# Recurrence on TensorE: a 64-column first half, a 64-partition second half, and two new step orders

## The chip, the cores and the metric

The kernel runs on one core of a Trainium2 chip. The metric is the device time of one execution in microseconds (us). The engines are named as the profile names them: PE (TensorE's matmuls) and PEld (its weight loads), DVE (VectorE), ACT (ScalarE), POOL (GpSimd) and SP (which issues the transfers).

## What is computed

A recurrence over 768 steps for 4 x 8 heads of size 40, then an attention mixture of experts, then a token and channel mixer. The change is in the recurrence:

```python
for t in range(S):
    y[:, :, t] = np.einsum('bhd,bhde->bhe', rt, state)
    Sa = np.einsum('bhde,bhe->bhd', state, at)
    state_decay = state * wt[:, :, None, :] - np.einsum('bhd,bhe->bhde', Sa, bt)
    state = state_decay + np.einsum('bhd,bhe->bhde', vt, kt)
```

## The kernel before, in words

The 768 steps are cut into 12 chunks of 64 steps, two chunks to a pair. The 32 heads lie in 11 groups of three (the last of two), and the groups in three quads (`QUADS`): 12, 12 and 8 heads. A step of the recurrence's program has a letter and a quad, for instance `z1`; in the text below a step of quad 1 is written z/1.

Inside a chunk the unknown row Sa depends on the rows before it, through a triangular 64x64 system for each head. It is solved in two halves of 32 rows. For one quad of one chunk the chain is:

- z (`z1`, line 275): old state times `a` into the PSUM tile `zu`, 64 partitions for the chunk's 64 rows; straight behind it the first t (`tv` with half 0, line 284): scores `sc` times values `vu`, added to rows 0 to 31. ACT then copies these rows, negated, into `zt0` (line 288).
- x (`xz`, line 297): the inverse of the diagonal block `xt` times `zt0`; ACT copies the result into `vu` (line 301). Below, x0 is the first half and x1 the second.
- t (`tv` with half 1, line 284): scores times values for rows 32 to 63, now with the first half's results in `vu`, called t1 below; ACT copies them into `zt1`; then x again for the second half.
- d (`ds`, lines 320 and 322): the new state into `ST`, which DVE writes (line 327), and s (`st`, line 336): its transpose.

In `vu` (128 partitions) one 64-partition half holds the chunk's values, the other one starts at zero (POOL memset, line 129) and takes the solved rows. The half of the solved rows is partitions 64 to 127 in even chunks and 0 to 63 in odd ones. A matmul writes 32 columns of the array for rows of one half, at array column 0 or 64 (first half) or 32 or 96 (second half); the heads of a quad alternate between the two sides (`sides`).

Beside this chain, PE makes the output of the chunk before: v (`vut`, line 361), r (`rs`, line 381), h (`hh`, line 351) and y (`yy`, line 394); scores c of the next pair (`scores`, line 204); k (`kbt`, line 251) and p (`ptt`, line 264). DVE masks the scores (lines 209 and 385), multiplies outputs (line 398), writes the state, makes the decays (`decay`, line 163 and others) and runs `solve`: a transpose into `tp` (line 225), 31 dependent double steps (lines 234 and 236) and a transpose into `xt` (line 239). `xt` of a pair is needed by the first x of the pair's even chunk, and `solve` can start when the last scores of that pair are masked and copied by ACT into `td` (line 217).

The strings `EVEN` and `ODD` (lines 34 and 35) give the order in which the steps of a chunk are emitted; the tile layer then places the instructions of all chunks on the engines, so the order on an engine is read from the built program. PSUM tiles come from small rings: three of `zu`, two each of `pm` and `psc`, one `y`.

Of the kernel before, what the change touches and what calls it, by code (L numbers as in the profile page):

```python
# [30 lines left out]
E = 40  # L31
FIRST = "p0 S p1 p2 L D k0 M V q0 q1 q2 k1 k2"
PN = (1, 1)
EVEN = "c0 c1 h0 v0 r0 v1 c2 z2 z0 D v2 y0 m1 x0 c3 z1 m2 s0 x1 x2 t0 r1 c4 c5 h1 t2 t1 y1 h2 r2 k0 k1 m0 c6 c7 x4 x3 c8 d0 c9 c10 c11 L s1 y2 d1 s2 x5 S k2 d2"
ODD = "h0 v0 z0 v1 A r0 x0 r1 y0 t0 h1 z1 M m2 v2 z2 x1 x3 y1 k0 r2 p0 x2 h2 p1 t1 m0 k1 k2 t2 L y2 x5 m1 s0 d0 p2 s2 s1 d2 x4 d1"
QUADS = [(0, 4), (4, 8), (8, 11)]

def sides(q, n):

    g0, g1 = QUADS[q]  # L40
    a, b, e = n * g0, n * (g0 + 2), min(n * g1, 32 if n > 1 else G)
    for i in range(b - a):
        yield a + i, 0, i
        if b + i < e:
            yield b + i, 1, i

def spans(q):

    g0, g1 = QUADS[q]
    return (0, 120 * g0, 240), (64, 120 * g0 + 240, min(120 * g1, 1280) - 120 * g0 - 240)  # L50
# [18 lines left out]
class Rec:  # L69
# [207 lines left out]
        s.tv(c, q, 0)  # L277

    def tv(s, c, q, half):
        nc = s.nc  # L280
        zu, sc, vu = s.T["zu", q], s.T["sc", c], s.T["vu", c]
        for h, b, i in sides(q, 3):
            o = 64 * b + 32 * half
            nc.tensor.matmul(zu[o:o + 32, 40 * i:40 * i + 40], sc[:, h, 32 * half:32 * half + 32],  # L284
                             vu[:, 40 * h:40 * h + 40], start=False, stop=True, skip_group_check=True)
        d = 64 * (1 - c % 2) + 32 * half
        for b, o, n in spans(q):
            nc.scalar.activation(s.zt[half][d:d + 32, o:o + n], zu[b + 32 * half:b + 32 * half + 32, :n], AF.Copy,  # L288
                                 scale=-1.0)
# [189 lines left out]
    def chunk(s, c):  # L479
# [34 lines left out]
        def solve():  # L514
            if even and p1:
                s.bg.append(s.solve(p + 1))

        def loads():
            s.rbd_load(c)
            if not last:  # L520
                s.load_r(c + 1)
            if c + 2 < 2 * n:
                s.load_chunk(c + 2)

        def load_next():
            if not even and p2:
                s.load_a(p + 2)
                s.load_kb(p + 2)

        def decay():  # L530
            if even and p2:
                s.bg.append(s.decay(p + 2))

        def scale():
            if not even and p2:
                while "pt" not in s.T[p + 2]:
                    s.pump(1)
                s.scale(p + 2)

        if even and p2:  # L540
# [4 lines left out]
                  S=lambda q: solve(), D=lambda q: decay(), L=lambda q: loads(), W=lambda q: c > 8 and next(s.cv, 0), A=lambda q: load_next(), M=lambda q: scale())  # L545
        for o in (EVEN if even else ODD).split():
            do[o[0]](int(o[1:] or 0))
# [590 lines left out]
```

## Time and profile before

| | us |
|---|---|
| median of 3 runs (lowest to highest) | 1063.22 (1062.9 to 1068.52) |
| profiled execution | 1056.61 |
| its span, first to last instruction | 1054.9 |
| recurrence within the span, to the last matmul of line 381 | about 451 |
| what follows (mixture of experts, mixers) | about 600 |

The recurrence is read by stages. A stage runs from the first x of one pair's even chunk to that of the next; these begin at 66.5, 163.3, 225.2, 290.8, 354.3 and 407.1 us of the span and are called stages 1 to 6 below. Stage 6 ends with the recurrence. The windows of the rows are cut a little earlier, where the transpose into `xt` starts. Matmuls in float32 stand as two records each in the trace, transposes as one.

### The profile page before, as it was taken

Reading aid. Unit: us, or ns where it says so; the run is one execution under the profiler, and the core shown is the slowest. Engines: PE = TensorE matmul, PEld = TensorE weight load, DVE = VectorE, ACT = ScalarE, POOL = GpSimd, SP = SyncE. Lnnn points to the kernel's source line nnn. Section 1 sums busy time; section 2 is a strip of 40 time slices with the busy share of each in tenths; the row PEclk is TensorE's granted clock in tenths of the full one; section 3 lists DMA queues with packets and bytes.
Section 4 is the critical chain, followed back from the end, with each engine's and each line's share of the span. In section 5 each row is a group of like instructions: output and inputs, shape, how many; then the busy total and the mean of one; then the engine's idle time right before and its main releaser. Section 6 shows DMA issues by size and latency. Waiting matters only on the chain.

```text
span 1054.9 us, 23653 instructions
## 1 busy us (share of the span) xinstructions
PE 944.2 (90%) x9378; PEld 814.6 (77%) x9378; DVE 675.0 (64%) x1793; ACT 481.9 (46%) x1250; POOL 169.7 (16%) x214
## 2 busy tenths in 40 slices
PE   2329889999999999967999999999998999999998
PEld 1327678887888888855877887888787898898887
DVE  6798697897988588648889777576287222222222
ACT  2225446646566565534667657666543121121211
POOL 5000000010000001343134142223254000000000
PEclk9758998999999999989999999999999999999999
DMA  9604424425243323465643441420262101101000
GB/s 175 133 2 95 102 49 107 91 79 133 50 105 79 97 61 99 138 196 137 159 116 89 124 115 31 98 61 26 86 203 63 56 1 56 34 21 56 1 25 25
DMA packets 101031, 88.84 MB, mean 84 GB/s; under 512 B 60785, under 2 KB 91073, under 8 KB 100321
## 3 DMA queue, kind: packets, MB, share of 16 engines
q1 hardware_dynamic: 100921, 87.34, 32.2%
q8 instruction: 74, 1.21, 0.5%
q14 instruction: 36, 0.29, 0.1%
HBM read 54.94 MB, written 15.73 MB: 67 GB/s over the span
## 4 chain that ended last, share of the span: by engine, by line
PE 65%; DVE 19%; DMA 7%; ACT 4%; issue 3%; SPq 2%; POOL 1%; DVEq 0%; ACTq 0%; POOLq 0%
PE pq L1031 11%; PE p L1045 11%; PE zu L284 3%; DVE pq L163 3%; PE psc L204 3%; PE psc L381 3%; PE po L858 3%; PE zu L297 3%; PE pq L832 2%; PE y L394 2%; PE pq L760 2%; PE pm L320 2%; PE pq L997 2%; PE pq L873 2%; PE pm L322 2%
## 5 line engine op out<-in xcount | busy, mean ns | idle before, releaser
L1035 DVE SCALAR_TENSOR_TENSOR hl<-pq,hh 128x512 fp32r<-128x512 f32 x72 | 49.6, 689 | 152.0 <-ACT hh L1034 152.0
L1034 ACT ACTIVATE hh<-pq 128x512 fp32r<-128x512 f32 x72 | 42.9, 596 | 190.9 <-PE pq L1031 190.9
L1045 PE MATMUL p<-c2h,hh 128*128 128x320 f32 x288 | 91.0, 316 | 3.4 <-DVE o L1048 3.4
L805 ACT ACTIVATE a<-s,nm 128x512 f32<-128x512 f32 (+3 forms) x128 | 68.7, 542 | 47.2 <-DVE nm L802 21.7
L1045 PE MATMUL p<-c2h,hl 128*128 128x320 f32 x288 | 89.5, 311 | 0.1
L1045 PE MATMUL p<-c2l,hh 128*128 128x320 f32 x288 | 89.4, 310 | 0.0
L297 PE MATMUL zu<-zt,xt 64*32 64x40 f32 x1536 | 43.2, 209 | 38.6 <-DVE pq L160 30.4
L301 ACT ACTIVATE vu<-zu 32x240 f32<-32x240 f32 (+1 forms) x144 | 48.5, 339 | 55.3 <-PE zu L297 45.6
L297 PEld LDWEIGHTS zu<-zt,xt 64*32 64x32 f32 x1536 | 37.3, 116 | 45.3 <-issue 37.0
L800 DVE TENSOR_REDUCE nm<-s 128x1 f32<-128x512 f32 (+3 forms) x128 | 61.9, 499 | 15.8 <-PE s L799 11.2
L288 ACT ACTIVATE zt<-zu 32x240 f32<-32x240 f32 (+1 forms) x144 | 48.6, 338 | 50.5 <-PE zu L284 48.8
L163 DVE TENSOR_TENSOR pq<-w,pq 120x88 f32<-120x88 f32 x186 | 61.0, 328 | 9.4 <-DMA w<-in_w 5.6
L818 POOL TENSOR_TENSOR a<-a,rs 128x128 f32<-128x128 f32 (+1 forms) x64 | 45.4, 731 | 126.6 <-DVE rs L813 90.6
L234 DVE TENSOR_TENSOR pr<-tp,x 128x31 f32<-128x31 f32 (+15 forms) x186 | 63.0, 339 | 3.9 <-DVE tp L225 0.5
L236 DVE TENSOR_TENSOR x<-x,pr 128x31 f32<-128x31 f32 (+15 forms) x186 | 63.3, 340 | 3.1
L1045 PEld LDWEIGHTS p<-c2h,hh 128*128 128x128 f32 x288 | 54.5, 189 | 7.7 <-DVE o L1048 5.0
L1031 PE MATMUL pq<-uh,c1h 128*128 128x512 f32 x144 | 57.5, 399 | 0.8 <-DVE ul L652 0.8
L1031 PE MATMUL pq<-uh,c1l 128*128 128x512 f32 x144 | 57.0, 396 | 0.0
L1045 PEld LDWEIGHTS p<-c2l,hh 128*128 128x128 f32 x288 | 54.5, 189 | 2.5
L1045 PEld LDWEIGHTS p<-c2h,hl 128*128 128x128 f32 x288 | 54.5, 189 | 0.3 <-DVE hl L1035 0.3
L204 PE MATMUL psc<-abd,kb 120*128 120x192 f32 (+1 forms) x242 | 51.1, 344 | 3.7 <-DVE sc L209 2.6
L284 PE MATMUL zu<-vu,sc 128*32 128x40 f32 x1536 | 50.8, 214 | 1.5 <-issue 0.8
(204 smaller groups left out, 2484.1 us busy)
## 6 DMA issues: line engine op xcount, KB each, us to landing
kb<-in_kb SPq DMA_DIRECT2D x5, 1320.0 KB
kh<-hb SPq DMA_DIRECT2D x64, 96.0 KB
cv<-in_c SPq DMA_DIRECT2D x18, 256.0 KB
w<-in_w SPq DMA_DIRECT2D x6, 660.0 KB
a<-in_a SPq DMA_DIRECT2D x6, 660.0 KB
r<-in_r SPq DMA_DIRECT2D x12, 330.0 KB
rbd<-in_r SPq DMA_DIRECT2D x36, 110.0 KB
vu<-in_v SPq DMA_DIRECT2D x12, 320.0 KB
```

Of the source, the lines that this page charges most:

```text
L163: e.tensor_tensor(two(pq, i + 1, x + 29 - 2 * i), two(t["w"], i, 31 - 2 * i), two(pq, i, x + 31 - 2 * i), OP.mult)
L204: nc.tensor.matmul(ps[:, n:n + nheads(g), :], t["kb"][:k, g, c % 2, :], abd[:k, g, :nheads(g), :], start=True, stop=True)
L234: v.tensor_tensor(prv, tp[:, j + 1:, j:j + 1].to_broadcast([128, n, j + 1]), x[:, j:j + 1, :j + 1].to_broadcast([128, n, j + 1]), OP.mult)
L236: v.tensor_tensor(x[:, j + 1:, :j + 1], x[:, j + 1:, :j + 1], prv, OP.subtract)
L284: nc.tensor.matmul(zu[o:o + 32, 40 * i:40 * i + 40], sc[:, h, 32 * half:32 * half + 32], vu[:, 40 * h:40 * h + 40], start=False, stop=True ...
L288: nc.scalar.activation(s.zt[half][d:d + 32, o:o + n], zu[b + 32 * half:b + 32 * half + 32, :n], AF.Copy, scale=-1.0)
L297: nc.tensor.matmul(zu[o:o + 32, 240 + 40 * i:280 + 40 * i], xt[r, h, :], s.zt[half][r, 40 * h:40 * h + 40], start=True, stop=True, skip_gr ...
L800: nc.vector.tensor_reduce(nm[:, x:x + 1], s, axis=AX.X, op=OP.max, negate=True)
L805: nc.scalar.activation(a[:, n0:n1], s, AF.Exp, bias=nm[:, -1:] if nb_ == 2 else nm[:, :1], accum_out=sm[:, x, i % 2:i % 2 + 1])
L1031: nc.tensor.matmul(p, l, r, start=(n == 0), stop=(n == 7))
L1035: nc.vector.scalar_tensor_tensor(hl, p, 0.0, hh, op0=OP.max, op1=OP.subtract)
L1045: nc.tensor.matmul(Y[s][i], hs[x][:, ts], w[:, k], start=(k + n == 0), stop=(k == 11 and n == 2))
```

## The change

`tv` with half 0 now multiplies all 64 columns of the scores, so it writes rows 0 to 63 of `zu` at once, over 128 partitions. The solved half of `vu` is zero at that time, so this adds the chunk's values for both halves. `tv` with half 1 then adds only what the solved first half gives to rows 32 to 63, over the 64 partitions that hold solved rows. The number of matmuls is the same. Both step orders are new.

```diff
-EVEN = "c0 c1 h0 v0 r0 v1 c2 z2 z0 D v2 y0 m1 x0 c3 z1 m2 s0 x1 x2 t0 r1 c4 c5 h1 t2 t1 y1 h2 r2 k0 k1 m0 c6 c7 x4 x3 c8 d0 c9 c10 c11 L s1 y2 d1 s2 x5 S k2 d2"
+EVEN = "m2 v0 h0 c0 z0 v1 c1 r0 c2 D v2 z2 x2 c3 m0 c4 x0 t2 z1 y0 x1 t1 c5 t0 h1 r1 r2 x3 y1 h2 c6 c7 k0 x5 c8 s0 c9 y2 x4 c10 c11 s2 d0 m1 S L d2 s1 k1 k2 d1"
...
     def tv(s, c, q, half):
...
+        u = 64 * (1 - c % 2)
+        r = slice(u, u + 64) if half else slice(0, 128)
+        m = 32 if half else 64
         for h, b, i in sides(q, 3):
             o = 64 * b + 32 * half
-            nc.tensor.matmul(zu[o:o + 32, 40 * i:40 * i + 40], sc[:, h, 32 * half:32 * half + 32],
-                             vu[:, 40 * h:40 * h + 40], start=False, stop=True, skip_group_check=True)
-        d = 64 * (1 - c % 2) + 32 * half
+            nc.tensor.matmul(zu[o:o + m, 40 * i:40 * i + 40], sc[r, h, 32 * half:32 * half + m],
+                             vu[r, 40 * h:40 * h + 40], start=False, stop=True, skip_group_check=True)
+        d = u + 32 * half
```

In the changed kernel lines 284, 297, 351, 381 and 394 are lines 288, 301, 355, 385 and 398, and `x` of the second half reads `zt_114`, of the first `zt_113`.

First place: PE at the start of an even chunk (chunk 4, counted from 0; its first x stands at 225.2 us in the trace before), from the first x on. Before:

```order
L297 MATMUL zu<-zt_113,xt 32x40 x32
L284 MATMUL zu<-vu,sc 32x40 x24
L351 MATMUL y<-S,r 64x120
L284 MATMUL zu<-vu,sc 32x40 x8
L351 MATMUL y<-S,r 64x80
L351 MATMUL y<-S,r 64x120
L297 MATMUL zu<-zt_114,xt 32x40 x12
L394 MATMUL y<-kbt,sr 64x40 x8
L297 MATMUL zu<-zt_114,xt 32x40 x20
L320 MATMUL pm<-vu,kbt 120x120
```

Now:

```order
L301 MATMUL zu<-zt_113,xt 32x40 x20
L288 MATMUL zu<-vu,sc 32x40 x8
L301 MATMUL zu<-zt_113,xt 32x40 x12
L355 MATMUL y<-S,r 64x120 x4
L385 MATMUL psc<-rbd,vut 128x192
L288 MATMUL zu<-vu,sc 32x40 x12
L385 MATMUL psc<-rbd,vut 128x192 x2
L288 MATMUL zu<-vu,sc 32x40 x12
L385 MATMUL psc<-rbd,vut 128x192 x2
L385 MATMUL psc<-rbd,vut 128x128
L398 MATMUL y<-kbt,sr 64x40 x12
L251 MATMUL pm<-ident,kb 128x120
```

The second half's t now starts between the x of the first half, output work of the chunk before stands between the links of the chain, and the first d comes later.

Second place: PE in the odd chunk behind it (chunk 5), around the z of quads 1 and 2. Before:

```order
L284 MATMUL zu<-vu,sc 32x40 x12
L275 MATMUL zu<-ST,a 64x120 x4
L284 MATMUL zu<-vu,sc 32x40 x12
L361 MATMUL pm<-ident,vu 120x128 x2
L351 MATMUL y<-S,r 64x120 x4
L361 MATMUL pm<-ident,vu 80x128
L275 MATMUL zu<-ST,a 64x120
L275 MATMUL zu<-ST,a 64x80
L275 MATMUL zu<-ST,a 64x120
L284 MATMUL zu<-vu,sc 32x40 x8
L297 MATMUL zu<-zt_113,xt 32x40 x12
```

Now:

```order
L275 MATMUL zu<-ST,a 64x120 x4
L288 MATMUL zu<-vu,sc 64x40 x12
L275 MATMUL zu<-ST,a 64x120
L275 MATMUL zu<-ST,a 64x80
L275 MATMUL zu<-ST,a 64x120
L288 MATMUL zu<-vu,sc 64x40 x8
L385 MATMUL psc<-rbd,vut 128x192 x4
L355 MATMUL y<-S,r 64x120
L301 MATMUL zu<-zt_113,xt 32x40 x8
L288 MATMUL zu<-vu,sc 32x40 x12
L301 MATMUL zu<-zt_113,xt 32x40 x12
```

The two z with their first t stand in a row and all write 64 rows, and a second half's t (32 rows) stands between two x.

Third place: DVE from the second transpose into `xt` on (163 us in the trace before). Before:

```order
L239 STREAM_TRANSPOSE xt<-x 128x32x32
L209 TENSOR_TENSOR sc<-psc,mask 128x384 x2
L163 TENSOR_TENSOR pq<-w,pq 120x2x44
L398 TENSOR_TENSOR ptt<-y,ptt 64x80
L163 TENSOR_TENSOR pq<-w,pq 120x2x44 x5
L165 TENSOR_TENSOR wp<-w,pq 120x44
L167 RECIPROCAL wr<-wp 120x44
L209 TENSOR_TENSOR sc<-psc,mask 128x384
L170 TENSOR_TENSOR pq<-pq,wr 120x22x32
L209 TENSOR_TENSOR sc<-psc,mask 128x384
L170 TENSOR_TENSOR pq<-pq,wr 120x22x32
L327 TENSOR_TENSOR ST<-pm,mf 120x480
```

Now, as far as the next transpose into `tp`:

```order
L239 STREAM_TRANSPOSE xt<-x 128x32x32
L209 TENSOR_TENSOR sc<-psc,mask 128x128
L163 TENSOR_TENSOR pq<-w,pq 120x2x44
L165 TENSOR_TENSOR wp<-w,pq 120x44
L167 RECIPROCAL wr<-wp 120x44
L170 TENSOR_TENSOR pq<-pq,wr 120x22x32 x2
L331 TENSOR_TENSOR ST<-pm,mf 120x480
L225 STREAM_TRANSPOSE tp<-td 128x1024
```

Most of the next pair's scores now stand ahead of this transpose into `xt`, inside the solve, and not behind it.

## Rows read from the trace of the kernel before

**Rows 1.** The page: busy time and share of the span; 40 equal slices, tenths.
```profile
PE 944.2 (90%) x9378; PEld 814.6 (77%) x9378; DVE 675.0 (64%) x1793; ACT 481.9 (46%) x1250; POOL 169.7 (16%) x214
PE   2329889999999999967999999999998999999998
```
**Rows 2.** Windows: stretch, its length, busy us (instructions) by engine, clock, DMA.
```profile
100.00:161.40 61.40, 53.28 (x704) 44.34 (x699) 49.61 (x139) 29.20 (x71) 2.70 (x4) 0.95 0.39 87
161.40:223.20 61.80, 59.97 (x944) 51.60 (x943) 50.46 (x135) 35.63 (x96) 3.82 (x6) 0.94 0.35 85
223.20:288.90 65.70, 62.11 (x992) 53.74 (x991) 55.95 (x149) 38.88 (x101) 4.57 (x6) 1.00 0.40 96
288.90:352.30 63.40, 61.06 (x978) 53.00 (x976) 53.18 (x132) 37.89 (x100) 3.82 (x6) 0.97 0.35 86
352.30:405.07 52.77, 51.41 (x909) 45.09 (x908) 38.11 (x98) 34.90 (x95) 2.27 (x3) 1.00 0.27 70
405.07:456.40 51.33, 47.74 (x853) 40.12 (x851) 33.71 (x61) 24.84 (x66) 16.15 (x10) 1.00 0.48 152
```
**Rows 3.** PE's waits: 100 to 161.4 us, then 161.4 to 288.9, then 288.9 to 405.
```profile
PE zu L297 <- issue: 2.5, 2, 1.8
PE y L351 <- DVE ptt L398: 1.9, 1, 1.9
...
PE zu L297 <- DVE xt L239: 1.8, 2, 1.1
...
PE zu L297 <- DVE xt L239: 2.1, 2, 1.6
```
**Rows 4.** Windows of two solves, from `tp` to the first x: columns as in rows 2.
```profile
122.00:163.00 41.00, 35.81 (x406) 30.27 (x406) 39.12 (x121) 15.65 (x38) 1.16 (x1) 0.95 0.22 52
241.00:291.00 50.00, 46.22 (x708) 39.19 (x710) 42.93 (x117) 27.57 (x74) 2.48 (x3) 1.00 0.43 98
```
**Rows 5.** Timeline of PE: start, length, line, tile, shape (rows*columns), records.
```profile
28.84 0.26 PE L284 MATMUL zu<-vu,sc 128*32 128x40 f32 x2
29.03 1.14 PE L204 MATMUL psc<-abd,kb 120*128 120x192 f32 x6
...
427.04 0.62 PE L297 MATMUL zu<-zt,xt 64*32 64x40 f32 x24
427.59 1.57 PE L381 MATMUL psc<-rbd,vut 120*128 120x192 f32 x8
429.09 0.90 PE L394 MATMUL y<-kbt,sr 128*64 128x40 f32 x24
429.91 0.62 PE L284 MATMUL zu<-vu,sc 128*32 128x40 f32 x24
430.47 0.63 PE L275 MATMUL zu<-ST,a 120*64 120x120 f32 x8
```
**Rows 6.** Timeline of PE, where neighbours have one shape and where not.
```profile
126.03 0.63 PE L351 MATMUL y<-S,r 120*64 120x120 f32 x8
126.50 0.85 PE L394 MATMUL y<-kbt,sr 128*64 128x40 f32 x24
...
134.28 0.63 PE L351 MATMUL y<-S,r 120*64 120x120 f32 x8
134.88 0.90 PE L336 MATMUL pm<-ident,ST 120*120 120x120 f32 x7
...
190.60 0.94 PE L297 MATMUL zu<-zt,xt 64*32 64x40 f32 x48
191.47 0.90 PE L394 MATMUL y<-kbt,sr 128*64 128x40 f32 x24
```
**Rows 7.** DVE: groups by line in 223.2 to 288.9 (busy us, mean ns).
```profile
L163 DVE TENSOR_TENSOR pq<-w,pq 120x88 f32<-120x88 f32 x32 | 10.7, 333 | 0.4
L209 DVE TENSOR_TENSOR sc<-psc,mask 128x384 f32<-128x384 f32 (+1 forms) x12 | 6.1, 512 | 0.7 <-PE psc L204 0.4
L398 DVE TENSOR_TENSOR ptt<-y,ptt 64x240 f32<-64x240 f32 (+1 forms) x12 | 4.5, 378 | 4.5 <-PE y L394 4.3
```

More of the change, by code (lines that the diff above doesn't have):

```diff
@@ L33 @@
 PN = (1, 1)
-EVEN = "c0 c1 h0 v0 r0 v1 c2 z2 z0 D v2 y0 m1 x0 c3 z1 m2 s0 x1 x2 t0 r1 c4 c5 h1 t2 t1 y1 h2 r2 k0 k1 m0 c6 c7 x4 x3 c8 d0 c9 c10 c11 L s1 y2 d1 s2 x5 S k2 d2"
-ODD = "h0 v0 z0 v1 A r0 x0 r1 y0 t0 h1 z1 M m2 v2 z2 x1 x3 y1 k0 r2 p0 x2 h2 p1 t1 m0 k1 k2 t2 L y2 x5 m1 s0 d0 p2 s2 s1 d2 x4 d1"
+EVEN = "m2 v0 h0 c0 z0 v1 c1 r0 c2 D v2 z2 x2 c3 m0 c4 x0 t2 z1 y0 x1 t1 c5 t0 h1 r1 r2 x3 y1 h2 c6 c7 k0 x5 c8 s0 c9 y2 x4 c10 c11 s2 d0 m1 S L d2 s1 k1 k2 d1"
+ODD = "A z0 x0 v0 v1 z1 z2 r0 h0 x2 t0 m1 x1 m2 s0 v2 r1 y0 h1 m0 r2 M y1 p0 L p1 p2 h2 y2 x3 t1 t2 d0 s2 k0 x5 s1 k1 x4 d2 k2 d1"
 QUADS = [(0, 4), (4, 8), (8, 11)]
```

## The prediction

> **What bounds the kernel now.** I read the page first: PE is busy 90% of the span, and the slices show it well short of full only in the first three, under 80 us, and mildly where the recurrence ends [rows 1]. The change touches the recurrence alone, so next come its stages, as windows [rows 2]: from 161 to 405 us PE is busy 234.6 of 243.7 us (the sum of four rows), so it bounds, with 9.1 us idle. From 100 to 161 us it idles 8.1 us. The waits tell for whom [rows 3]: the largest after "issue" are for outputs (line 398) and for `xt`, the end of the solve on DVE. So a second bound runs close behind: the solve. In the solve from 122 us DVE is busy 39.1 of 41.0 us, so DVE sets its end; in the one from 241 us it is busy 42.9 of 50.0 us, and PE 46.2 [rows 4]: the longest wait for `xt` there is 1.1 and 1.6 us [rows 3], so PE and the solve end nearly together. A change must be added up on PE, and then held against the solve.
>
> **Prices.** All from full-clock stretches. One float32 matmul of line 284 alone is two records, one behind the other, and with what surrounds it takes 0.19 us (28.84 to 29.03); 24 records, a quad on two sides of the array, take 0.56 us (429.91 to 430.47) [rows 5]. A quad is 12 slots of two records side by side (the last quad, 8 heads with 6 on one side, too), so a slot is (0.56 - 0.19)/10 = 0.037 us, and 0.12 us is constant. Line 394, the same 128 partitions and 40 columns but 64 columns of weights, takes 0.82 us (429.09 to 429.91): a slot of (0.82 - 0.12)/12 = 0.058. Line 297, 64 partitions and 32 columns, takes 0.55 us, like line 284 [rows 5]. The constant belongs to a change of tile shape: four heads of line 351 take 0.47 us when line 394 follows, which has its shape, and 0.60 us when full-width line 336 does [rows 6], so a change costs 0.13 us; I take 0.12. Other steps, by start to start or busy time: r and c 0.34 us a matmul (1.50 us for four, less one change), h 0.12, y 0.058, transposes (s, k) 0.12 [rows 5, 6].
>
> **The change part by part, on PE.** *64 columns in the first half.* 12 chunks x 3 quads x 12 slots = 432 slots, each (0.82 - 0.56)/12 = 0.022 us longer: +9.5 us. Line 394 is the same form, so the bounds are near: 8 and 10.
>
> *64 partitions in the second half.* Line 297 has this form now and takes what line 284 takes: 0.
>
> *Tile shapes.* In z and its first t, both now 64 columns wide, no change of shape is left between them, and the second half's t has the shape of x. Counted through the recurrence in the two orders as built, PE changes shape 358 times before and 287 times now: 71 x 0.12 = -8.5 us. Two pairs of rows give this price, so I allow a third to either side: -6 and -12.
>
> These three give +1.0 us, between -4 (8 - 12) and +4 (10 - 6): the new widths eat what the fewer shape changes give.
>
> The Trainium skill, TensorE: Matmul & The Clock Gate, section LDWEIGHTS, speaks against the change: a weight load takes a time that goes with the columns alone, and the partitions do not matter. Rows 5 agree in kind (64 partitions save nothing); by its figure 32 more columns are an estimated 27 ns a slot, not 22, so the part would be +11.5 and the three +3.0 us. I keep the rows' value.
>
> *The order moves work between stages.* Counting matmuls between the first x of one even chunk and of the next gives the differences below; each stage with two chunks also carries +1.6 us of widths (72 slots).
> Stage 1: 7 scores, 4 h, 3 s more, 4 k fewer, 10 shape changes fewer: 2.4 + 0.5 + 0.4 - 0.5 - 1.2 + 1.6 = +3.2.
> Stage 2: 7 scores, 6 r, 8 h, 12 y, 7 s and 4 k fewer, 28 shape changes fewer: -4.4 - 1.0 - 0.7 - 1.3 - 3.4 + 1.6 = -9.2.
> Stage 3: 13 shape changes fewer: 0. Stage 4: 3 h and 12 shape changes fewer: -0.2.
> Stage 5: 3 h, 12 y, 2 r, 7 k more, 7 shape changes fewer: 0.4 + 0.7 + 0.7 + 0.8 - 0.8 + 1.6 = +3.4.
> Stage 6 (one chunk of widths): 4 h, 4 s, 4 r, 1 k more, one change fewer: +3.2.
> The widths of chunk 0 lie under the first solve, where PE stands idle.
>
> **Held against the solve.** Stage 1 ends with a solve that DVE sets, so PE's +3.2 us do not count there; DVE's own list does. Between `tp` and `xt` it now holds 5 more score masks, one more output mask, one output product and one decay step: at 0.47, 0.47, 0.36 and 0.3 us (means less what overlaps [rows 7]) +3.4 us. DVE had 1.9 us idle in that window [rows 4], so the bounds are +1.5 and +3.4, and `tp` itself stands behind some 0.7 us more output work on PE: I take +3.
> Stage 2: DVE now has little between `xt` and the next `tp` (third place), so the solve starts early, held only by the first d; -9.2 us stays with PE, with bounds of -6 and -10.6.
> Stages 3 and 4: between `tp` and `xt` DVE has 7 instructions fewer (two decay steps, one score mask, two output masks, three products, against one state write): -2.7 us. But `tp` comes later: ahead of the state write in front of it PE has 4 h, 6 r, 12 y, 4 k, 3 s more and four d fewer (four records each, at 0.12), +2.1 us. The two cancel: 0, within 2 us for each stage.
> Stage 5: +3.4 less the wait for `xt` that now lies under PE's work, some 0.8: +2.6. Stage 6 has no solve: +3.2.
>
> **Sum.** 3 - 9.2 + 0 - 0.2 + 2.6 + 3.2 = -0.6 us. The profiled execution is 1056.6 us, its span 1054.9; the median of the runs is 1063.2, so the profile lies 0.6% below it. I put the difference on the median: 1062.6 us. Stage bounds that fall together give about -8 and +8, so its own range is 1055 to 1071 us. 0.5% (5.3 us) is about what a measurement of this kernel can tell from no change, so this is "same".
>
> **Rivals.** *The waits go (faster).* The new order spreads the chain: r, h, y and k stand between x, t and the second x (first place), scores come in ones to fours and not in sixes, and both z stand in a row. PE's idle time was 8.1 us from 100 to 161 and 9.1 us to 405 [rows 2]. If half of the 17 us goes: -9, with the sum 1054. For it: 2.5 us of "issue" waits at x [rows 3] stood where x and t were packed together. Against it: the `xt` and output waits are DVE's, and the DVE list is not shorter.
>
> *The solve becomes the bound (slower).* If DVE, in its new order, waits for PE inside the solve so that the 2.7 us are not won while `tp` still comes 2.1 us later, and PE reaches the first x as early as before, each of stages 3, 4 and 5 grows by 2.1 us or more, and stage 2, whose solve starts no earlier than its first d, gives back some 3: +9, 1072 us. It decides from a solve of more than some 47 us (the one from 241 us takes nearly 50). For it: in the 50 us window DVE had 7 us idle [rows 4], and in that stage 4.3 us of idle ahead of line 398 alone ended with PE [rows 7]; the new list has such links too. Against it: fewer instructions.
>
> *Tiles side by side (faster).* x and the second half's t now share a shape and write different strips. If neighbouring bursts ran beside each other, some 23 bursts of t (12 slots, 0.43 us) would vanish under x: -10, 1052 us. The trace speaks against it: 48 records of line 297, x of a first half and then x of a second half in other strips, take 0.87 us (190.60 to 191.47) [rows 6], which is 24 slots, one burst behind the other. The Trainium skill, TensorEngine Tiling (Array Packing), section Tiling Modes, says that tiles operate independently and that different tiles can execute loads and matmuls in parallel; it bears on this rival alone, and that row does not show it across bursts.
>
> **How the numbers follow.** Forecast 0.45, waits go 0.25, solve bounds 0.25, side by side 0.05. The first rival, the third and the lowest edge of the forecast are faster than 1057.9 us: 0.33. The second and the highest edge are slower than 1068.5: 0.26. Same: 0.41. The range takes both rivals' values: 1051 to 1072.
>
> **What would show it.** In the profile after: first t at about 0.82 us a quad (right) or nearer 0.56 (the width costs nothing); z and the t behind it about 0.1 us closer; the second half's t at 0.55; the first x at about 166, 219, 284, 348 and 403 us; waits of PE for `xt` of at most 2 us a pair. Wrong would be: waits at x of several us (the solve bounds), PE's idle time from 100 to 405 us down by half, or a quad of t that vanishes beside x.

## The result, and the profile after

The changed kernel took 1050.34 us (median of five runs) against 1062.9 us for the one before: a ratio of 0.9878, 95% interval 0.9836 to 0.9919, so faster by 1.2%. The forecast was 1062.6 us and "same"; the time lies just below the range of 1051 to 1072 us. Two later comparisons gave 0.9937 (0.9905 to 0.9969) and 0.9907 (0.9873 to 0.9941); why they differ is part of what follows.

The profiled execution took 1048.28 us, against 1056.61 before. In the page after, PE's busy time hardly fell (before 944.2, [rows 1]):

```profile
PE 940.7 (90%) x9378; PEld 819.4 (78%) x9378; DVE 672.3 (64%) x1793; ACT 480.1 (46%) x1250; POOL 167.0 (16%) x214
```

The stages as windows, columns as in [rows 2]: stretch, length, busy us (instructions) of PE, PEld, DVE, ACT and POOL, granted clock, DMA share and GB/s.

```profile
100.00:159.40 59.40, 53.66 (x729) 46.23 (x728) 53.39 (x152) 29.79 (x73) 2.70 (x4) 0.98 0.35 82
159.40:216.40 57.00, 53.68 (x838) 49.41 (x840) 44.11 (x116) 33.14 (x91) 3.72 (x6) 0.85 0.35 84
216.40:277.70 61.30, 60.34 (x991) 53.38 (x988) 55.95 (x149) 37.38 (x99) 3.86 (x6) 1.00 0.42 101
277.70:340.20 62.50, 60.45 (x984) 53.05 (x979) 53.88 (x134) 37.38 (x99) 3.82 (x6) 1.00 0.37 88
340.20:396.20 56.00, 55.19 (x945) 48.70 (x943) 40.16 (x104) 35.85 (x95) 2.27 (x3) 1.00 0.27 69
396.20:447.20 51.00, 49.99 (x912) 43.46 (x907) 31.51 (x62) 26.72 (x70) 14.44 (x10) 1.00 0.49 148
```

Two things to see. Stage 3 (the third line) is 4.4 us shorter with as many PE instructions, 991 for 992. And in stage 2 the granted clock is 0.85, against 0.94 before [rows 2]. PE's waits, from 100 to 159.4 us and then from 159.4 to 277.7 (answering [rows 3]):

```profile
PE y L355 <- DVE ptt L402: 2.2, 2, 1.2
PE psc L204 <- DVE sc L209: 1.6, 2, 0.9
...
PE zu L301 <- DVE xt L239: 2.9, 2, 2.6
PE zu L288 <- issue: 1.3, 1, 1.3
```

The 2.5 us of "issue" waits at x in stage 1 are gone; there is a 2.6 us wait for the second `xt`, at the end of stage 1.

**Where the time went.** I split each stage into work, clock and waits. For every step from one matmul's start to the next I took the mean of the steps between the same lines and shapes at full clock over the profiles of this study, long ones left out; the sum of these is the work. What a step at half clock takes beyond that, up to as much again, is the clock; the rest is waiting. Between work and waits this is good to some 3 to 4 us over the recurrence: with other limits for what counts as long, the work changes by -1 to -6 us and the waits by -4 to -9. Stage 6 ends here with the last y matmul (455.5 us before, 447.1 after).

| stage | before | after | change | forecast | of the change: work | clock | waits |
|---|---|---|---|---|---|---|---|
| 1 | 96.8 | 94.3 | -2.4 | +3 | +2.8 | -2.1 | -3.1 |
| 2 | 61.9 | 57.2 | -4.7 | -9.2 | -8.9 | +4.0 | +0.2 |
| 3 | 65.6 | 61.2 | -4.4 | 0 | -0.1 | 0 | -4.3 |
| 4 | 63.6 | 62.5 | -1.0 | -0.2 | -0.8 | -1.0 | +0.9 |
| 5 | 52.7 | 56.0 | +3.3 | +2.6 | +2.4 | 0 | +0.8 |
| 6 | 48.4 | 48.8 | +0.4 | +3.2 | +3.0 | 0 | -2.7 |
| sum | 388.9 | 380.1 | -8.8 | -0.6 | -1.6 | +0.7 | -8.0 |

The column of work is the forecast's list for PE almost stage by stage (+3.2, -9.2, 0, -0.2, +3.4, +3.2). What the forecast did not have is the last two columns. By stage it missed by -5.4, +4.5, -4.4, -0.8, +0.7 and -2.8 us, so the clock in stage 2 hides half of what stages 1 and 3 gained.

Each run also lists its span and mean granted clock. The clock has two levels, 1.2 and 2.4 GHz (0.5 and 1.00 in the profile), so a run spent 2 x (1 - clock) x span at half clock; "half clock" below is this time. Over the 219 runs of this study, each kernel against its own mean, a run is 0.375 us longer for every us at half clock (correlation 0.89). The table has the median time, the half-clock time, and the median brought to 90 us of half clock at that price. Ten runs, over 1.5% above the fastest of their kernel, count as slow and are in this table and the price alone; without them the price is 0.34 and no entry of the last column moves by more than 1.3 us.

| kernel | runs | median us | half clock: median (range) | at 90 us |
|---|---|---|---|---|
| before | 89 | 1062.4 | 97 (78 to 122) | 1059.8 |
| changed, three comparisons | 5, 12, 10 | 1050.3, 1059.5, 1052.9 | 88, 111, 98 (84 to 148) | 1050.7, 1051.9, 1051.5 |
| new orders, old t (twice) | 6, 6 | 1050.2, 1050.9 | 85, 86 (82 to 95) | 1051.3, 1051.8 |
| old orders, new t | 6 | 1078.4 | 131 (127 to 143) | 1062.9 |
| only the even order new | 10 | 1057.4 | 90 (75 to 133) | 1056.3 |
| only the odd order new | 12 | 1065.5 | 104 (93 to 120) | 1060.3 |
| old orders, wide first half | 12 | 1064.9 | 100 (89 to 111) | 1060.0 |
| old orders, short second half | 8 | 1070.7 | 122 (104 to 135) | 1059.3 |
| changed, old t in the last pair | 6 | 1049.4 | 85 (80 to 90) | 1051.7 |
| changed, 14 matmuls added | 12 | 1056.1 | 96 (73 to 119) | 1053.5 |
| changed, 20 matmuls added | 10 | 1050.6 | 80 (67 to 104) | 1053.6 |
| before, without loads | 10 | 1059.4 | 88 (80 to 98) | 1060.8 |
| old orders, new t, without loads | 5 | 1071.8 | 118 (104 to 131) | 1061.4 |

The kernel before, taken from each comparison alone, comes to 1058.2 to 1061.2 us in the last column, so rows of different comparisons can be held against each other to some 3 us. At equal half clock the change is worth some 8 us, all three times; against the kernel before of the same comparison, which is known for the later two, 9.3 and 9.5. What is added to or taken from that is the clock.

### The profile page after: what moved, and what is told of

The parts are those of the page before. It is cut to its first block, busy times and chain, and to the rows that moved or that the text cites. A ratio compares the mean times of both kernels' runs of the same rounds, so it can differ in the third digit from the quotient of the medians.

```text
span 1046.5 us, 23651 instructions
## 1 busy us (share of the span) xinstructions
PE 940.7 (90%) x9378; PEld 819.4 (78%) x9378; DVE 672.3 (64%) x1793; ACT 480.1 (46%) x1250; POOL 167.0 (16%) x214
## 4 chain that ended last, share of the span: by engine, by line
PE 68%; DVE 17%; DMA 7%; ACT 3%; issue 3%; POOL 1%; SPq 0%; DVEq 0%; ACTq 0%; POOLq 0%
PE p L1049 10%; PE pq L1035 10%; PE psc L385 4%; PE psc L204 3%; PE zu L288 3%; PE po L862 3%; DVE pq L163 3%; PE pq L836 3%; PE zu L301 3%; PE pq L764 3%; PE pq L1001 2%; PE pm L324 2%; PE pq L877 2%; PE y L398 2%; PE pq L988 2%
## 5 line engine op out<-in xcount | busy, mean ns | idle before, releaser
L1039 DVE SCALAR_TENSOR_TENSOR hl<-pq,hh 128x512 fp32r<-128x512 f32 x72 | 49.6, 689 | 152.0 <-ACT hh L1038 152.0
L305 ACT ACTIVATE vu<-zu 32x240 f32<-32x240 f32 (+1 forms) x144 | 48.8, 339 | 70.4 <-PE zu L301 64.0
L301 PE MATMUL zu<-zt,xt 64*32 64x40 f32 x1536 | 48.4, 211 | 34.6 <-DVE pq L160 30.4
L301 PEld LDWEIGHTS zu<-zt,xt 64*32 64x32 f32 x1536 | 40.2, 117 | 41.8 <-issue 35.4
L822 POOL TENSOR_TENSOR a<-a,rs 128x128 f32<-128x128 f32 (+1 forms) x64 | 45.6, 734 | 127.0 <-DVE rs L817 94.5
L288 PE MATMUL zu<-vu,sc 64*32 64x40 f32 (+1 forms) x1536 | 60.6, 219 | 3.0 <-ACT vu L305 1.7
L288 PEld LDWEIGHTS zu<-vu,sc 64*32 64x32 f32 (+1 forms) x1536 | 53.1, 127 | 7.5 <-ACT vu L305 3.7
L385 PE MATMUL psc<-rbd,vut 120*128 120x192 f32 (+1 forms) x264 | 54.8, 341 | 1.5 <-DVE sr L389 1.3
```

What stands on the lines that cost most here:

```text
L288: nc.tensor.matmul(zu[o:o + m, 40 * i:40 * i + 40], sc[r, h, 32 * half:32 * half + m], vu[r, 40 * h:40 * h + 40], start=False, stop=True, ...
L301: nc.tensor.matmul(zu[o:o + 32, 240 + 40 * i:280 + 40 * i], xt[r, h, :], s.zt[half][r, 40 * h:40 * h + 40], start=True, stop=True, skip_gr ...
L305: nc.scalar.activation(vu[d:d + 32, o:o + n], zu[b + 32 * half:b + 32 * half + 32, 240:240 + n], AF.Copy)
L385: nc.tensor.matmul(ps[:, n:n + nheads(g), :], vt[:k, g - g0, :], rbd[:k, g, :nheads(g), :], start=True, stop=True)
L1039: nc.vector.scalar_tensor_tensor(hl, p, 0.0, hh, op0=OP.max, op1=OP.subtract)
```

## Experiments

**Orders and widths apart.** The theory: the new orders took waits away, and widths and shape changes nearly cancel. The rival: the new t gave the gain. First the new orders with the old `tv`:

```diff
-EVEN = "c0 c1 h0 v0 r0 v1 c2 z2 z0 ...
+EVEN = "m2 v0 h0 c0 z0 v1 c1 r0 c2 ...
-ODD = "h0 v0 z0 v1 A r0 x0 ...
+ODD = "A z0 x0 v0 v1 z1 z2 ...
```

> The new step orders with t as it was before (32 columns, 128 partitions). As built, PE changes tile shape 374 times (before 358, after 287). Theory 'the orders took waits away': PE's work is 16 x 0.12 = +1.9 us against before and its long waits in the recurrence fall from 30.7 us to about 23 us as in after, so the recurrence ends some 5 to 7 us sooner: ratio to before about 0.993 to 0.995 of the whole, long waits at about 23 us. Rival 'the new widths gave the gain': the ratio is 1.000 to 1.002 and the long waits stay near 31 us.

Measured: 0.9879 (0.9848 to 0.9911), as much as the whole change, and more than the 0.993 to 0.995 expected; at equal half clock, with 85 us against 100 in this comparison, it is 8 us. By the split, waits fell from 36 to 24 us and work rose by 4; with other limits for long steps, waits fall by 6 to 10 and work changes by -2 to +2. Then the new `tv` in the old orders, of which these are two lines:

```diff
+        r = slice(u, u + 64) if half else slice(0, 128)
+        m = 32 if half else 64
```

> The new t (64 columns in the first half, 64 partitions in the second) in the old step orders. Shape changes as built: 312. Theory 'the orders took waits away': widths +9.5 us, 46 shape changes fewer at 0.12 = -5.5 us, so +4 us on PE with the waits near 31 us: ratio 1.002 to 1.004. Rival 'the new widths gave the gain': ratio 0.988 to 0.993. The first t reads 0.82 us a quad by the prediction's price, the second 0.55.

Measured: 1.0154 (1.0121 to 1.0186), +16 us where +4 was expected, and nothing of the rival. Work is +2 us, near the forecast; 19 us more lie in the clock, 15 to 16 of them in four windows of stages 3, 5 and 6, which were at full clock before [rows 2]:

```profile
234.00:245.00 11.00, 10.83 (x196) 9.56 (x189) 7.58 (x22) 7.00 (x20) 1.57 (x4) 0.59 0.43 123
...
272.00:284.00 12.00, 10.74 (x113) 9.76 (x114) 4.62 (x10) 4.85 (x14) 0.00 (x0) 0.57 0.35 78
...
370.00:385.00 15.00, 14.29 (x252) 13.25 (x251) 4.28 (x10) 7.13 (x20) 1.11 (x2) 0.77 0.45 126
...
427.00:445.00 18.00, 17.84 (x277) 15.92 (x277) 10.74 (x21) 7.54 (x21) 4.32 (x3) 0.62 0.48 147
```

PE at the first of them, in the timeline of this kernel (start, length, line, tile, shape, records, and in brackets the wait ahead of it):

```profile
233.25 1.47 PE L301 MATMUL zu<-zt,xt 64*32 64x40 f32 x64 [0.70 <-DVE xt L239]
234.76 1.39 PE L288 MATMUL zu<-vu,sc 64*32 64x40 f32 x48
236.08 0.66 PE L355 MATMUL y<-S,r 120*64 120x120 f32 x2
```

And at the same place in the kernel before:

```profile
225.17 1.47 PE L297 MATMUL zu<-zt,xt 64*32 64x40 f32 x64 [0.70 <-DVE xt L239]
226.69 1.38 PE L284 MATMUL zu<-vu,sc 128*32 128x40 f32 x48
228.00 0.42 PE L351 MATMUL y<-S,r 120*64 120x120 f32 x2
```

Same wait, same sequence, same times, but t over 64 and not 128 partitions; behind it the same y matmuls take 0.66 us and not 0.42, since the clock is at half from 236.0 us on. So a second theory, to be tested below: a stretch of nothing but 64-partition tiles behind a wait exposes the clock to a fall. Each order alone, with the new t:

> The new t, the new order for even chunks and the old one for odd chunks. Shape changes 327. If the gain belongs to one list: the order of even chunks holds the scores c, the solve S and the first x of a pair, so the waits for xt and the place of the transpose into tp go with it; theory 'the orders took waits away' gives this kernel most of the gain, a ratio near 0.992. If the gain belongs to the odd list (z and t in a row, A first), the ratio is near 1.000.

> The new t, the old order for even chunks and the new one for odd chunks. Shape changes 294, so PE's work alone is +9.5 - 7.7 = +1.8 us against before. By the theory that the even list carries the waits: ratio 1.000 to 1.002. If the odd list carries the gain: near 0.990, with the issue waits at 104 to 113 us gone because the loads of a and kb are issued earlier.

Measured: the even order alone 0.9933 (0.99 to 0.9965), the odd alone 1.0022 (0.9992 to 1.0052). The even order holds the waits: 28 us by the split, as in the changed kernel, against 41 with the odd order alone. The odd one then takes 40 shape changes away (327 to 287 as built), -4.8 us at 0.12; at equal half clock the step from even alone to both is some -5 us, across comparisons.

**Which half brings the clock down.** In the old orders, one half of the new t at a time, first the wide first half, then the short second half (either leaves the sums of rows 32 to 63 changed):

```diff
-        r = slice(u, u + 64) if half else slice(0, 128)
+        r = slice(0, 128)
...
-        m = 32 if half else 64
+        m = 32
```

> Old step orders; the first half's t with 64 columns as in the change, the second half's t still over all 128 partitions (so the chunk's own values count twice in rows 32 to 63: part of the computation is changed). Both new halves in the old orders gave half clock for 89.6 us of the recurrence from the first x on, against 38.0 us before, and +16 us. Theory 'the 64-partition t in the packed x and t lets the granted clock fall': here the half-clock time stays near before's 38 us (35 to 50), and only the widths count: +9.5 - 37 x 0.12 = +5 us, ratio 1.003 to 1.007. Rival 'the wider first half brings the falls': half-clock time near 90 us, ratio near 1.015.

> Old step orders; the first half's t with 32 columns as before, the second half's t over the 64 partitions of solved rows only (so the chunk's own values are left out of rows 32 to 63). Theory 'the 64-partition t in the packed x and t lets the granted clock fall': half-clock time 60 to 90 us as with both new halves (before 38.0), ratio 1.008 to 1.015 although PE's work is no more than before (7 shape changes fewer, -0.8 us). Rival 'the wider first half brings the falls': half-clock time 35 to 50 us, ratio 0.998 to 1.002.

Measured: the wide first half 1.0029 (1.0009 to 1.0049), half clock 100 us a run, near the 98 us of before in this comparison; the short second half 1.009 (1.0058 to 1.0123), half clock 122 us, and 1 us slower than before once that is taken out. So in the old orders the 64-partition half, which is hardly slower by itself, costs its time through the clock. Whether the tiles do this by themselves is open: in the profile of the short second half PE stands in "issue" waits for 5.0 us at x around 107 and 116 us, against 1.4 with the wide first half and 2.5 before, and further down a fall of the clock goes when such waits go, with the same t. The profiles alone would not have told it: their half-clock times from the first x on were 54 and 56 us, both above before's 38, and the runs decided.

**Does idle PE cost the clock in stage 2?** The changed kernel with matmuls added where PE waits:

```diff
+                d = s.nc.tensor.matmul(s.wm[:, 256:496], s.ident, s.mask[:, None, :60].to_broadcast([128, 4, 60]),
+                                       start=True, stop=True, skip_group_check=True)
```

> The changed kernel with 14 matmuls added that nothing reads (128 partitions x 128 columns x 240, about 0.4 us each), where PE waits between 152 and 161 us for the end of the second solve. The granted clock was at half from 156.5 to 173.6 us there, of which PE was at work from 161.3 us on. Theory 'the clock fell because PE stood idle, and stage 2 pays for it': the half-clock stretch goes, stage 2 (57.2 us) loses 4 to 6 us, ratio to before 0.982 to 0.985 (changed kernel 0.988). Rival 'the solve or the chain of stage 2 sets its length': stage 2 stays within 1 us, ratio 0.987 to 0.989. Nine shape changes more give back 1 us in either case.

> As the kernel with 14 added matmuls, and 6 more behind the last x of chunk 0, where PE waits from 74.0 to 79.8 us at half clock and then works on at half clock to 88 us. Theory 'PE at half clock sets the start of the second solve': the transpose into tp (117.9 us in the changed kernel) comes 2 to 4 us sooner and stage 1 with it, ratio 0.978 to 0.982. Rival 'DVE sets stage 1': stage 1 stays within 1 us of the kernel without the 6, ratio the same as there.

(They write beside `y` in its PSUM bank, and `y`'s sums change with it.) Windows of the changed kernel, ahead of stage 2 and in it, and then of the one with 14 added, with its stage 3:

```profile
148.00:161.00 13.00, 6.88 (x51) 5.05 (x50) 12.72 (x42) 1.06 (x3) 0.00 (x0) 0.83 0.35 102
161.30:218.50 57.20, 55.54 (x874) 50.94 (x875) 44.28 (x116) 33.86 (x93) 3.73 (x7) 0.86 0.35 81
```
```profile
148.00:161.00 13.00, 10.90 (x73) 8.88 (x74) 12.75 (x43) 1.06 (x3) 0.02 (x1) 1.00 0.35 101
161.90:213.30 51.40, 48.22 (x811) 42.98 (x810) 44.13 (x115) 32.45 (x91) 3.91 (x8) 0.97 0.38 87
213.30:281.00 67.70, 66.08 (x1046) 58.21 (x1046) 55.96 (x146) 38.49 (x101) 3.46 (x5) 0.97 0.40 93
```

The clock held and stage 2 lost 5.8 us, as the theory said. But some 3 us of that is work that the scheduler now put into stage 3, where the clock fell elsewhere; stages 2 and 3 together take 119.1 us against 118.4. Ratio 0.9922 (0.9886 to 0.9958), half clock 90 us a run: no gain, and both expected ratios missed. With 6 more in stage 1 the ratio was 0.9896 (0.9857 to 0.9934) and stage 1 took 95.5 us, not less than the 94.5 with 14, as the rival had it. Its half clock was 80 us a run, the least of all kernels; the added matmuls took back what that gave (table).

**The "issue" waits.** In the trace, instruction transfers of 16 KB each, taken here to be PE's, end near where these waits begin (one runs from 103.77 to 105.10 us in the trace of before; PE stops at 104.96 and goes on at 106.72). So it is with all 31 "issue" waits of PE over 0.4 us in the recurrence, in 15 of the profiles: PE goes on 1.2 to 2.2 us after such a transfer has ended, in 30 of them 1.2 to 1.8, while the transfers of before come 9 us apart in the mean. This speaks for late instructions as the cause; what makes them late is the question. Without the loads beside them, shown for `kb`, and so for `a` and `w`, with the order on PE held:

```diff
-        s.nc.sync.dma_start(kb, s.in_kb[p].rearrange("p g c x t -> p g c (x t)"))
+        s.nc.gpsimd.memset(kb, 0.0) if p == 2 else s.nc.sync.dma_start(kb, s.in_kb[p].rearrange("p g c x t -> p g c (x t)"))
```

> The kernel before with the same order on PE, but the loads of a, kb and w of the third pair (2.6 MB, under way from 97 to 116 us, DMA share 0.83) are left out: POOL writes constants instead, so the values of that pair and all behind it differ. Theory 'the issue waits at the packed x and t are late instruction loads, held up behind these transfers': the 2.5 us of issue waits at x between 104 and 113 us go, to under 0.5 us, and the second tp (122.3 us) comes some 2 us sooner. Rival 'the packed small matmuls use up instructions faster than any load brings them': the issue waits stay between 1.5 and 3 us.

> The new t in the old step orders, same order on PE, without the loads of a, kb and w of the third pair (POOL writes constants instead, so values differ). There PE waited 3.6 us for issue at x between 106 and 116 us and the granted clock was at half from 109.7 to 119.9 us. Theory 'late instruction loads behind these transfers': the issue waits go to under 0.5 us, the half-clock stretch at 110 us with them, the second tp (126.8 us) comes 4 to 6 us sooner. Rival 'packed small matmuls alone': issue waits of 2 to 4 us stay, and the half-clock stretch too.

PE's waits from 100 to 120 us: first the new t in old orders with its loads, then the kernel before without them.

```profile
PE zu L301 <- issue: 3.6, 2, 2.1
```
```profile
PE zu L297 <- issue: 1.5, 1, 1.5
PE zu L284 <- ACT vu L301: 1.0, 1, 1.0
```

From the kernel before 1.0 of 2.5 us went and `tp` came 1.0 us sooner (ratio 0.9981, 0.9957 to 1.0005): the theory misses, and the 1.5 us left are at the lower edge of the rival. With the new t all 3.6 us went, the half clock at 110 us with them (clock 1.00 from 98 to 118 us, 0.79 with the loads), and `tp` came at 119.6, not 126.8; ratio 1.0076 (1.0036 to 1.0115). The loads have a part in it; whether the packed small matmuls alone can outrun their instructions stays open.

**Is it the chip or the 64-partition t?** The changed kernel again:

> The changed kernel once more, unchanged, for the spread of its half-clock time. Theory 'the clock sets the spread': the runs lie on a line against the time that each spent at half clock, some 0.38 us a us, like the others; and the half-clock time of the whole execution is 85 to 95 us in the median against 98.5 before.

It gave 0.9937, with 109 us of half clock in the median and not the 85 to 95 expected. Its profile shows, at the first x of the last pair, the same instructions at another clock. Windows of 9 us from there, first profile and this one:

```profile
398.30:407.30 9.00, 8.67 (x216) 7.42 (x217) 7.08 (x16) 4.78 (x14) 2.65 (x2) 1.00 0.32 94
```
```profile
397.80:406.80 9.00, 8.68 (x166) 7.16 (x166) 5.14 (x12) 4.07 (x12) 1.38 (x1) 0.61 0.23 42
```

Stage 6 took 57.7 us there, not 48.8. So I ran three kernels side by side: the new orders with the old t, the changed kernel, and the changed kernel with the old t in the last two chunks:

```diff
+        old = c >= 10
+        r = slice(u, u + 64) if half and not old else slice(0, 128)
+        m = 32 if half or old else 64
```

> The new step orders with the t of before, once more, beside the changed kernel on one chip. Theory 'the 64-partition t exposes stage 6 to a fall of the granted clock': this kernel, whose t runs over 128 partitions, has no half-clock stretch at the first x of the last pair; its half-clock time over the whole execution is 80 to 95 us in the median, some 10 to 25 us less than the changed kernel's, and at 0.38 us a us it is 3 to 9 us faster: about 1050 us, ratio 0.987 to 0.990. Rival 'the falls come by the chip and not by the t': both kernels have the same half-clock time and the same ratio within 0.3%.

> The changed kernel, for the same comparison on one chip. Theory 'the 64-partition t exposes stage 6': half-clock time 95 to 115 us in the median, runs in two groups (with and without some 20 us of half clock at the first x of the last pair), median 1053 to 1060 us. Rival 'the falls come by the chip': the same time as the kernel with the t of before, within 0.3%.

> The changed kernel with the t of before (32 columns, 128 partitions) in the last two chunks only, where the fall at 400 us stands. 15 shape changes more and two chunks of the wider first half less: +1.8 - 1.4 = about 0 us of work. Theory 'the 64-partition t exposes stage 6': half-clock time 82 to 95 us in the median, near 1050 us. Rival: as the changed kernel.

Measured: 0.9887 (0.9855 to 0.9918), 0.9907 (0.9873 to 0.9941) and 0.9876 (0.9847 to 0.9905); runs from 1048.9 to 1053.5, from 1047.4 to 1059.9 and from 1047.6 to 1051.9 us; half clock 86, 95 and 85 us. The changed kernel's best runs are as good as any; with 128-partition t at that one place its upper end is gone. Over 18 runs, no kernel with the new orders and the old t there passed 1054 us; of 24 runs of the changed kernel 12 did, 3 of 9 in this comparison.

This does not settle it. The first two ratios lie within 0.3%, as the rival had it, and all three intervals overlap; half clock and the upper end speak for the theory. Eight of the 12 runs above 1054 us come from the second comparison, made on another chip, beside which no kernel with the old t ran, so the chip may have a part in it. The last kernel looks steadier, and its median is the lowest of all; that it is faster is not shown.

## Why the prediction was wrong

In short: the work on PE was priced rightly, but the sum kept the waits as they were. It put DVE's waits inside the third solve, and PE's ahead of the second `tp`, at no change; the new orders took most of both away.

- **The list for PE: right.** First t at 0.76 us a quad where z and y, of its shape, stand beside it (396.17 to 396.93; nine other such quads 0.67), the forecast having 0.82 with a change of shape and so 0.70 without; the second at 0.55, as priced:

```profile
396.17 0.87 PE L288 MATMUL zu<-vu,sc 128*64 128x40 f32 x23
396.87 0.23 PE L398 MATMUL y<-kbt,sr 128*64 128x40 f32 x1
396.88 0.23 PE L288 MATMUL zu<-vu,sc 128*64 128x40 f32 x1
396.93 0.87 PE L398 MATMUL y<-kbt,sr 128*64 128x40 f32 x23
...
402.04 0.62 PE L288 MATMUL zu<-vu,sc 64*32 64x40 f32 x24
402.59 0.43 PE L385 MATMUL psc<-rbd,vut 120*128 120x192 f32 x1
```

  The net was +1.0 (-4 to +4) and came out at -1.6, by a split good to 3 to 4 us; by it the orders alone, the widths alone and each half alone lie within 4 us of the same prices.
- **Stage 1: wrong by its start, the largest miss.** The forecast let `tp` come 0.7 us later; it came 4.4 us sooner (117.9 for 122.3 us), 4.8 counted from the first x. PE's waits from 100 to 120 us before were these:

```profile
PE zu L297 <- issue: 2.5, 2, 1.8
PE psc L204 <- DVE sc L209: 1.1, 1, 1.1
```

  After, no wait ahead of `tp` there is over 0.4 us. The even order brings it: `tp` comes at 118.5 us with the even order alone, at 118.2 with both orders and the old t, and at 128.6 with the odd order alone. From there to the first x it is 2.4 us longer, against +3.
- **Stage 2: work right (-8.9 for -9.2), clock missing.** 15.7 us of the stage lie at half clock, 6.1 before, which costs 4.0 us more.
- **Stage 3: the failing step.** I counted DVE's instructions inside the solve (-2.7 us) and let it keep its waits. `tp` did come later, by 2.6 us against the first x (forecast 2.1), but the solve, from `tp` to the start of the transpose into `xt`, shrank by 7.0, from 47.6 to 40.6 us. DVE's longest waits in it before, 241.2 to 288.8 us, and after, 237 to 277.7:

```profile
DVE ptt L398 <- PE y L394: 3.8, 3, 1.8
DVE ST L327 <- PE pm L322: 1.3, 1, 1.3
```
```profile
DVE sr L389 <- PE psc L385: 0.3, 1, 0.3
DVE sc L209 <- PE psc L204: 0.3, 1, 0.3
```

  5.1 us of waiting for PE's y and d stood in the middle of the solve, and the new order takes it out. It is the orders that do so: with both orders and the old t, 0.2 us of it is left and the stage takes 61.4 us; with the new t in the old orders 9.5 us of it stand there, part of them at half clock. The prediction had the row (4.3 us ahead of line 398, [rows 7]) and used it only in the slower rival, as a sign that such waits might grow.
- **Stages 4 to 6.** -1.0 for -0.2 and +3.3 for +2.6; stage 6 +0.4 for +3.2, with 2.7 us of waits gone. Of these, 1.6 us were waits for loads of the part behind the recurrence, which stood ahead of the last y; to the last matmul of line 381, where the rows let the stage end, it grew by 2.7 us.
- **Rivals.** "The waits go" was the case: -9 with the sum was forecast, -8.3 us came in the profile and some -8 at equal half clock. That the size fits is in part luck. Its own sign, PE's idle time down by half, did not come: from 100 us to the end of stage 5 it went from 17.2 to 12.9 us, since it grew in stage 2, while 2.7 us of the waits that went lie in stage 6, outside its count. "The solve becomes the bound" did not happen: from `tp` to the first x the third solve takes 42.7 us (before 49.6), well under its 47. "Side by side" did not either: 40 records of t and x in one shape, interleaved, take 0.75 us (399.65 to 400.40), which is 20 slots of 0.037.
- **From profile to median: a term that was not there.** I put the profile's difference on the median. The profiled execution of before had 84 us of half clock, against 97 in the median of its runs; at 0.375 that is some 5 of the 6 us by which it lay below. So the range was built about a time whose spread is mostly the clock's, and nothing in it was the clock's. The -12.6 us between the medians of the first comparison are more than the 8 to 9 us of the change at equal half clock; the clock of the kernel before is not known there.
- **Weight loads.** The Trainium skill, TensorE: Matmul & The Clock Gate, section LDWEIGHTS, was weighed for its rule that partitions do not matter to a weight load. The trace agrees: a load of 32 columns takes 109 ns over 64 partitions and 113 over 128, and one of 64 columns 138. The quads agree too, at 0.55 us each; in the old orders the partitions matter through the granted clock.
- **The price of the clock.** The Trainium skill, TensorE: Matmul & The Clock Gate, section Terms, takes half of the time at half clock as its cost. These runs give 0.375. A part of that time may lie where PE waits anyway; how much of the difference this makes was not measured.

## What to carry to other kernels

Add up the busy engine's work, but list also the waits that stand inside a chain on another engine (here DVE's, inside the solve) and ask of each whether the new order keeps it: here the work moved by some 2 us and the waits by some 8. Before a median is forecast from one profile, read the granted clock of every run: the changed kernel's runs lay up to 14 us apart, and their half clock 33 us, worth 12 of the 14 at 0.375. Where small tiles follow a wait and all partitions cost no more time than half of them, as in t here, keep all: in the old orders this was worth some 22 us of half clock a run, in the new ones it is likely but not settled.

## What the runs showed of the hardware

- One sequence at one place (the first x of the last pair of the changed kernel) ran at full clock in two profiles and at half clock for 20.5 us in a third, where that stage took 57.7 and not 48.8 us. With the new orders and t over 128 partitions there, no profile of three shows a fall.
- A matmul over 64 partitions took no less time than one over 128 (0.55 us a quad each), yet in the old orders the kernel with the 64-partition t alone had 122 us of half clock a run, that before 98 and that with the wide first half alone 100.
- A change of tile shape cost 0.13 us where neighbours could be read [rows 6]. Over a kernel, 0.12 us each fits: 71 fewer changes cancelled the wider first half, and the odd order with 40 fewer gave some 5 us, though it changes more than the shapes.
- Where PE stopped in the recurrence with nothing to wait for that the profile shows, for 0.4 to 3.3 us, it went on 1.2 to 2.2 us after a 16 KB instruction transfer had ended (31 waits in 15 profiles). Without the loads beside them, 1.5 of 2.5 us stayed in one kernel and none of 3.6 us in the other.
